# Expert weights loaded as fp16 by converting transfers on GpSimd's queue, in an attention and mixture-of-experts kernel

## The chip, the cores and the metric

One NeuronCore of a Trainium2 chip runs the whole program. Its engines are named here as the profile names them: PE (TensorE; PEld is its weight load), DVE (VectorE), ACT (ScalarE), POOL (GpSimd) and SP (SyncE, which only issues transfers here). Each works through its own instructions in order and waits on semaphores for the others. The metric is the device time of one execution in microseconds (us); lower is better.

## The reference

A cross attention between 512 tokens and 32 state rows for each of 8 x 8 (batch, head) pairs, then a dense mixture of 8 experts whose token weights come from eight rounds of Sinkhorn normalisation:

```python
scores = scale * x @ state.T                 # per batch and head, S=512, Ns=32, D=64
xread = softmax(scores) @ state
sread = softmax(scale * state @ x.T) @ x
x = concat([xread, sread])                   # as 4352 tokens x 512
P = exp(x @ w_gate - max)                    # 4352 x 8
for _ in range(8):
    P /= P.sum(1) + 1e-9; P /= P.sum(0) + 1e-9; P *= N / E
out = sum(P[:, e] * (relu(x @ w1[e]) @ w2[e]) for e in range(8))   # w1: 512x1024, w2: 1024x512
```

Inputs and output are fp32. The weights of one expert are 2 MB (w1) and 2 MB (w2); all matmuls of the kernel on large operands take fp16.

## The kernel before

The 4352 tokens are nine blocks: eight of 512 (the xread rows of one batch) and one of 256 (all sread rows). xread is never formed for the experts: aT holds the attention weights, the state is kept as a block-diagonal bdT, and for each expert and batch `project` multiplies bdT by w1 into V, so that the first expert layer is V times aT ("hidden", tile hps).

The program has two stages.

*First stage.* Attention of all batches, the gate, Sinkhorn, all of expert 0, and the first layer of expert 1 for its first two blocks are described as operations (`Op`) with a rank (a due time), the engines that may run each with planned durations, and what they depend on. `issue` (L48) plans by list scheduling: it repeatedly takes the operation that can start first by the plan, lower rank first among equals, and emits it. That fixes the order of instructions on every engine, SP's and POOL's queues too; at run time semaphores alone decide when each runs. The due times are `due_x` (L354, attention, for each half batch), `due_e` (L355, blocks of expert 0) and `due_1` (L356, the start of expert 1). Rows that the text speaks of:

- x comes in 16 pieces of 512 KB (`x_st`, two buffers, L441) on SP's queue, in 1 KB runs. The two pieces of batch 0 are cast to fp16 (`x_nat`) on DVE and ACT, the others on POOL (L454).
- `weights_ops` (L463) loads an expert's weights on SP in eight fp32 pieces of 512 KB into three staging buffers (`wst`), each cast to fp16 on ACT or DVE (L376, L378: the helper `copy`). It is called for experts 0 and 1 (L496, L497). So 16 pieces, and a piece is asked for only when the cast of the third one before it is done.
- POOL also runs the normalisation of the attention weights (`normA`, L577, tile a16), one for each half batch.
- Expert 0: `project_ops` (w1 and bdT into v_ps, copied to V), `hidden_mul` (V and aT into hps), a ReLU eviction into hT, then the second layer (hT and w2 into yps) and a copy into acc. Expert 0's result stays unscaled in acc.

*Expert loop (from L874).* For experts 1 to 7 and the nine blocks, the second layer of one block is interleaved with the first layer of the next and the projection of the one after. The second layer is a Strassen-like scheme with seven products of half size: it needs differences of parts of w2 (tile T, eight subtractions on DVE an expert, L196), sums of parts of the hidden matrix (tile sm, DVE, L277 to L280), and a copy of the first product A into a PSUM tile Bseed (ACT, L323) for which PE waits. The products are accumulated into acc on DVE (L312), scaled by the token's weight. In the pass of expert 1, acc is first scaled by expert 0's weight, half on ACT (L318), half on DVE (L320).

- `load_w` (L159) is a generator that brings in the next expert's weights: each step of it issues one fp32 piece on SP into the staging pool (`moe_wst`, three buffers) and casts the piece of two steps before on ACT (L181). Ten steps bring the eight pieces; the next eight steps make one T subtraction each.
- `step` (L875) is called after each part of the work, and every sixth call takes one step of the generator. The generator starts in block 1 of an expert (L886), and what is left of it is done after block 6 (L901).
- The fp16 weights have two buffers (`moe_w`), so an expert's load waits until the one two before is no longer read.

Of the kernel before, what the change touches and what calls it, by code (L numbers as in the profile page):

```python
# [9 lines left out]
FP32 = mybir.dt.float32  # L10
# [77 lines left out]
def kernel(  # L88
# [9 lines left out]
    nc = tc.nc  # L98

    B, H, S, D = x.shape  # L100
# [53 lines left out]
    mwst = ctx.enter_context(tc.tile_pool(name="moe_wst", bufs=3))  # L154
# [4 lines left out]
    def load_w(e, engines):  # L159
# [4 lines left out]
        casts = []  # L164
        n = NKC + NFB // 2
        for k in range(n + 2):
            if k < n:
                if k < NKC:
                    st = mwst.tile([128, F], FP32, name="w1st", tag="wst")
                    nc.sync.dma_start(out=st, in_=w1r[e, :, k, :])  # L170
                    casts.append((w1h[:, k, :], st))
                else:
                    g = k - NKC
                    st = mwst.tile([128, 2, Dm], FP32, name="w2st", tag="wst")
                    nc.sync.dma_start(out=st, in_=w2r[e, :, ds(g * 2, 2), :])
                    casts.append((w2h[:, ds(g * 2, 2), :], st))
            if k >= 2:
                dst, src = casts[k - 2]
                eng = engines[(k - 2) % len(engines)]
                if eng is nc.scalar:  # L180
                    nc.scalar.copy(out=dst, in_=src)  # L181
                else:
                    eng.tensor_copy(out=dst, in_=src)
            yield
# [20 lines left out]
    axs = actx.enter_context(tc.tile_pool(name="attn_xs", bufs=2))  # L205
# [148 lines left out]
    due_x = lambda u: 10.0 + 5.54 * u  # L354
    due_e = lambda bi: 25.1 + 13.7 * bi  # L355
    due_1 = 150.0  # L356
# [29 lines left out]
    def dma(rank, kb, emit, after=(), takes=()):  # L386
        return op(rank, {"DMA": (kb / 330.0, kb / 330.0 + 2.2)}, lambda _: emit(), after, takes)

# [50 lines left out]
    for b in range(B):  # L439
        for g in range(2):  # L440
            st = slot(axs, 2, [128, H // 2, NSC * D], FP32, "x_st")  # L441
# [21 lines left out]
    def weights_ops(e, rank, on):  # L463
        w1 = slot(mw, 2, [128, NKC, F], FP16, "w1h")
        w2 = slot(mw, 2, [128, NFB, Dm], FP16, "w2h")
        wslots[e] = (w1, w2)
        for k in range(NKC + NFB // 2):
            first = k < NKC
            st = slot(mwst, 3, [128, F], FP32, "wst")

            def load(k=k, st=st):
                if k < NKC:
                    nc.sync.dma_start(out=st.tile, in_=w1r[e, :, k, :])
                else:
                    nc.sync.dma_start(out=st.tile.rearrange("p (a b) -> p a b", a=2),
                                      in_=w2r[e, :, ds((k - NKC) * 2, 2), :])

            def cast(eng, k=k, st=st):
                if k < NKC:
                    copy(eng, w1.tile[:, k, :], st.tile)  # L480
                else:
                    copy(eng, w2.tile[:, ds((k - NKC) * 2, 2), :],
                         st.tile.rearrange("p (a b) -> p a b", a=2))

            d = dma(rank + (k,), 512, load, [w_ready.get((e, k - 1))] if k == 1 else [], [st])
            takes = [w1] if k == 0 else [w2] if k == NKC else []
            before = [w_ready[e, 0]] if 0 < k < NKC else [w_ready[e, NKC]] if k > NKC else []
            w_ready[e, k] = op(rank + (k,), on, cast, [d] + before, takes, [st])

    def w1_ready(e):  # L490
        return [w_ready[e, k] for k in range(NKC)]

    def w2_ready(e):
        return [w_ready[e, k] for k in range(NKC, NKC + NFB // 2)]
# [440 lines left out]
```

## Time and profile before

| | us |
|---|---|
| median of 3 runs | 794.11 |
| lowest and highest run | 793.38, 795.03 |
| the profiled execution's own time | 794.67 |
| its span, first to last instruction | 792.9 |

| stretch of the profiled execution | from, us | to, us |
|---|---|---|
| first stage (to the Bseed start matmuls, L871) | 0 | 165.0 |
| expert loop | 165.0 | 792.9 |

The granted TensorE clock was 0.995 over the span. The groups of weight casts, as busy time and number of instructions:

| casts | engine | busy us | count |
|---|---|---|---|
| w1h, w2h in the loop (L181) | ACT | 25.2, 25.1 | 24, 24 |
| w1h, w2h in the first stage (L376) | ACT | 5.3, 4.2 | 5, 4 |
| w1h, w2h in the first stage (L378) | DVE | 2.1, 4.2 | 3, 4 |

SP's queue carries 51.14 of the 52.46 MB that are moved. Median times from issue to landing of a 512 KB piece: 5.1 us for x_st, 6.1 us for wst in the first stage, 3.6 us for the pieces in the loop. In lines of the profile, "xN" is the number of instructions in a group, the first two numbers of a line of the timeline are start and duration in us, and a bracket at the end tells how long the engine was idle before and what ended it. A window's line gives the busy time in it of PE, PEld, DVE, ACT and POOL, with the instructions in brackets, then PE's clock, the share of time that the DMA engines were busy, and GB/s. A busy time of PE counts a matmul with its latency, so that PE can be "busy" and not at its peak.

### The profile page before, as it was taken

The numbers are of one execution on the slowest core, as the hardware profiler recorded it, in microseconds if no ns is written. First come the engines' busy times: TensorE is split into PE (matmuls) and PEld (weight loads), VectorE is DVE, ScalarE is ACT, GpSimd is POOL, SyncE is SP. The second block draws the span as 40 slices with busy tenths as digits, with TensorE's granted clock in tenths as the row PEclk, the third lists the DMA queues.
The fourth block names the chain that finished last, engine by engine and source line by source line (L and its number), as shares of the span: only waits on it lengthen the run. The fifth ranks groups of instructions, "written<-read, shape, count | busy, mean of one in ns | idle before, by whom it ended". The sixth has DMA issues, their size and how long they took to land.

```text
span 792.9 us, 16564 instructions
## 1 busy us (share of the span) xinstructions
PE 764.5 (96%) x6593; PEld 514.2 (65%) x6593; DVE 648.8 (82%) x1603; ACT 566.7 (71%) x1072; POOL 39.5 (5%) x80
## 2 busy tenths in 40 slices
PE   4899999989999999999999999999999999999996
PEld 3455554556667666766667666766667766767675
DVE  7898877787898888978788888978788888978885
ACT  5787776568977688577866688578866688576662
POOL 1543210000000000000000000000000000000000
PEclk9999999999999999999999999999999999999999
DMA  8874000002400033001410033001400030002233
GB/s 280 288 253 138 1 2 1 1 1 64 125 28 1 1 104 111 1 2 54 129 33 2 1 107 107 1 2 54 133 28 2 1 107 28 1 24 97 95 107 134
DMA packets 29535, 52.46 MB, mean 66 GB/s; under 512 B 4625, under 2 KB 12817, under 8 KB 29457
## 3 DMA queue, kind: packets, MB, share of 16 engines
q1 hardware_dynamic: 28368, 51.14, 20.3%
q8 instruction: 51, 0.84, 0.4%
q10 hardware_dynamic: 1088, 0.26, 0.2%
q14 instruction: 28, 0.22, 0.1%
HBM read 42.48 MB, written 8.91 MB: 65 GB/s over the span
## 4 chain that ended last, share of the span: by engine, by line
PE 63%; DVE 4%; ACT 2%; issue 0%; DVEq 0%
PE hps L252 22%; PE Bseed L298 16%; PE E L298 11%; PE A L298 10%; PE v_ps L237 3%; DVE acc L312 2%; ACT Hm L271 2%; DVE sm L277 1%; ACT w2h L181 1%; DVE sm L280 0%; DVE Hm L278 0%; DVE T L196 0%; DVE sm L279 0%; ACT w1h L181 0%; DVE acc L320 0%
## 5 line engine op out<-in xcount | busy, mean ns | idle before, releaser
L271 ACT ACTIVATE Hm<-hps 128x512 f16<-128x512 f32 (+1 forms) x488 | 262.3, 575 | 149.8 <-PE hps L252 138.9
L298 PEld LDWEIGHTS <-Hm 128*128 128x128 f16 x1904 | 185.4, 98 | 74.4 <-issue 3.9
L252 PE MATMUL hps<-aT,V 128*128 128x512 f16 x864 | 230.5, 379 | 0.0
L312 DVE SCALAR_TENSOR_TENSOR acc<-Bseed,Pmat,acc 128x256 f32<-128x256 f32 x357 | 156.9, 479 | 57.1 <-PE Bseed L298 53.6
L298 PEld LDWEIGHTS <-sm 128*128 128x128 f16 x1428 | 134.4, 98 | 54.9 <-DVE sm L277 24.4
L298 PE MATMUL Bseed<-T,Hm 128*128 128x256 f16 x952 | 124.5, 273 | 2.7 <-DVE acc L312 2.5
L298 PE MATMUL A<-w2h,Hm 128*128 128x256 f16 x952 | 126.1, 273 | 0.5
L252 PEld LDWEIGHTS <-V 128*128 128x128 f16 x864 | 84.5, 98 | 44.4
L241 ACT CAST V<-v_ps 128x512 f16<-128x512 f32 x216 | 111.0, 608 | 0.0
L312 DVE SCALAR_TENSOR_TENSOR acc<-E,Pmat,acc 128x256 f32<-128x256 f32 x238 | 104.4, 478 | 5.4 <-PE E L298 1.0
L277 DVE TENSOR_TENSOR sm<-Hm 128x512 f16<-128x512 f16 (+1 forms) x122 | 49.9, 409 | 21.6 <-ACT Hm L271 20.8
L298 PE MATMUL E<-T,sm 128*128 128x256 f16 x476 | 64.4, 274 | 0.7
L781 PE MATMUL yps<-w2h,hT 128*128 128x512 f16 x272 | 64.6, 379 | 0.0
L312 DVE SCALAR_TENSOR_TENSOR acc<-A,Pmat,acc 128x256 f32<-128x256 f32 x119 | 52.4, 479 | 15.0 <-PE A L298 14.9
L298 PE MATMUL Bseed<-T,sm 128*128 128x256 f16 x476 | 62.3, 272 | 2.3 <-ACT Bseed L323 2.3
L298 PE MATMUL E<-w2h,sm 128*128 128x256 f16 x476 | 62.3, 273 | 0.0
L278 DVE TENSOR_TENSOR Hm<-Hm 128x512 f16<-128x512 f16 (+1 forms) x122 | 50.0, 410 | 4.2
L280 DVE TENSOR_TENSOR sm<-Hm,sm 128x512 f16<-128x512 f16 (+1 forms) x122 | 50.0, 410 | 4.2
L279 DVE TENSOR_TENSOR sm<-sm,Hm 128x512 f16<-128x512 f16 (+1 forms) x122 | 49.1, 403 | 0.0
L323 ACT COPY Bseed<-A 128x512 f32<-128x512 f32 (+1 forms) x63 | 34.7, 552 | 18.7 <-PE A L298 15.6
L781 PEld LDWEIGHTS <-hT 128*128 128x128 f16 x272 | 24.8, 98 | 27.5 <-issue 2.6
L746 PE MATMUL hps<-aT,V 128*128 128x512 f16 x160 | 41.1, 389 | 0.4
(114 smaller groups left out, 626.1 us busy)
## 6 DMA issues: line engine op xcount, KB each, us to landing
w1st<-in_moe_w_dram SPq DMA_DIRECT2D x24, 512.0 KB, 3.6
w2st<-in_moe_w_dram SPq DMA_DIRECT2D x24, 512.0 KB, 3.6
x_st<-in_x_dram SPq DMA_DIRECT2D x16, 512.0 KB, 5.1
wst<-in_moe_w_dram SPq DMA_DIRECT2D x16, 512.0 KB, 6.1
out_dram<-acc SPq DMA_DIRECT2D x32, 256.0 KB, 3.1
out_dram<-acc SPq DMA_DIRECT2D x8, 64.0 KB, 1.7
st_st<-in_state_dram ACTq DMA_DIRECT2D x4, 64.0 KB, 3.2
st_st<-in_state_dram SPq DMA_DIRECT2D x4, 64.0 KB, 3.0
```

Of the source, the lines that this page charges most:

```text
L241: nc.scalar.copy(out=V[:, q, cols], in_=ps[q])
L252: nc.tensor.matmul(out, lhs, rhs, start=(k == 0), stop=(k == len(terms) - 1))
L271: nc.scalar.activation(out=Hm[:, i, j, :tn], in_=hps[:, :tn], func=AF.Relu)
L277: nc.vector.tensor_add(s1, a21, a22)
L278: nc.vector.tensor_sub(a21, a11, a21)
L279: nc.vector.tensor_sub(s2, s1, a11)
L280: nc.vector.tensor_sub(s4, a12, s2)
L298: nc.tensor.matmul(dst[:, c], lhs(j, c), rhs[:, j], start=first and c == 0 and j == 0, stop=(j == NJ - 1), skip_group_check=True)
L312: nc.vector.scalar_tensor_tensor(out=dst, in0=src[:, c], scalar=p[:, k], in1=dst, op0=ALU.mult, op1=ALU.add)
L323: nc.scalar.copy(out=Bb[:, :nk], in_=A[:, :nk])
L746: nc.tensor.matmul(ps.tile[:, :tn], lhs, rhs, start=(k == 0), stop=(k == len(terms) - 1))
L781: nc.tensor.matmul(yps.tile, hT[fb].tile[:, ds(tk * 128, 128)], w2h[:, fb, :], start=(fb == 0), stop=(fb == NFB - 1))
```

## The change

All weight loads move from SP's queue to POOL's, as 1 MB transfers that read fp32 and write fp16 directly into w1h and w2h: four an expert, 32 in all, in place of 64 of 512 KB. The staging pool and all 64 casts are gone. In the first stage, `dma16` books an issue on POOL (1.0 us in the plan) and then a transfer. The x staging gets a third buffer. The due times are others: 5.77 for 5.54, 27.5 and 14.7 for 25.1 and 13.7, and `due_1` 100 for 150; expert 1's weights are due at 50 (120 before). In `load_w`, four steps issue the four transfers, three steps do nothing, and the T subtractions follow.

The list scheduler makes of it, as the built program shows: SP's queue holds the state, then all 16 pieces of x with nothing between, and at the end the output. POOL's queue begins, after the masks, with five transfers and no wait between them: expert 0's first half of w1, expert 0's first half of w2, expert 1's first half of w1, expert 1's first half of w2, and then expert 0's second half of w1. (In the plan a second half may be issued only when the first half's transfer is done, a first half at once.) Then come the first normalisation, expert 0's second half of w2, and the x cast of batch 1; the two second halves of expert 1 stand among later x casts. On PE, the same matmuls as before stand in another order: expert 1's first layer for its two blocks no longer ends the stage, but stands among the second-layer matmuls of expert 0, twelve of which stand between the last two Sinkhorn sums.

```diff
--- before.py
+++ after.py
@@ -151,7 +151,6 @@
     outx = [out[b * SB:b * SB + S, :].rearrange("(p sc) d -> p sc d", sc=NSC) for b in range(B)]
     outs = [out[b * SB + S:(b + 1) * SB, :] for b in range(B)]
 
-    mwst = ctx.enter_context(tc.tile_pool(name="moe_wst", bufs=3))
     mw = ctx.enter_context(tc.tile_pool(name="moe_w", bufs=2))
     gsb = ctx.enter_context(tc.tile_pool(name="gate_sb", bufs=2))
     vpool = ctx.enter_context(tc.tile_pool(name="vpool", bufs=3))
@@ -161,26 +160,13 @@
         w1h = mw.tile([128, NKC, F], FP16, name="w1h", tag="w1h")
         w2h = mw.tile([128, NFB, Dm], FP16, name="w2h", tag="w2h")
         w16[e] = (w1h, w2h)
-        casts = []
-        n = NKC + NFB // 2
-        for k in range(n + 2):
-            if k < n:
-                if k < NKC:
-                    st = mwst.tile([128, F], FP32, name="w1st", tag="wst")
-                    nc.sync.dma_start(out=st, in_=w1r[e, :, k, :])
-                    casts.append((w1h[:, k, :], st))
-                else:
-                    g = k - NKC
-                    st = mwst.tile([128, 2, Dm], FP32, name="w2st", tag="wst")
-                    nc.sync.dma_start(out=st, in_=w2r[e, :, ds(g * 2, 2), :])
-                    casts.append((w2h[:, ds(g * 2, 2), :], st))
-            if k >= 2:
-                dst, src = casts[k - 2]
-                eng = engines[(k - 2) % len(engines)]
-                if eng is nc.scalar:
-                    nc.scalar.copy(out=dst, in_=src)
-                else:
-                    eng.tensor_copy(out=dst, in_=src)
+        for k in range(2):
+            nc.gpsimd.dma_start(out=w1h[:, ds(2 * k, 2)], in_=w1r[e, :, ds(2 * k, 2), :])
+            yield
+        for k in range(2):
+            nc.gpsimd.dma_start(out=w2h[:, ds(k * NJ, NJ)], in_=w2r[e, :, ds(k * NJ, NJ), :])
+            yield
+        for _ in range(3):
             yield
         if e:
 
@@ -202,7 +188,7 @@
 
     mh = ctx.enter_context(tc.tile_pool(name="moe_h", bufs=10))
     actx = ExitStack()
-    axs = actx.enter_context(tc.tile_pool(name="attn_xs", bufs=2))
+    axs = actx.enter_context(tc.tile_pool(name="attn_xs", bufs=3))
     axp = actx.enter_context(tc.tile_pool(name="attn_x", bufs=3))
     axt = actx.enter_context(tc.tile_pool(name="attn_xt", bufs=2))
     asb = actx.enter_context(tc.tile_pool(name="attn_sb", bufs=2))
@@ -351,9 +337,9 @@
 
 
     ops = []
-    due_x = lambda u: 10.0 + 5.54 * u
-    due_e = lambda bi: 25.1 + 13.7 * bi
-    due_1 = 150.0
+    due_x = lambda u: 10.0 + 5.77 * u
+    due_e = lambda bi: 27.5 + 14.7 * bi
+    due_1 = 100.0
     rings = {"bank": Ring(8)}
     EVICT16 = {"DVE": (0.36, 0.48), "ACT": (0.50, 0.66)}
     EVICT32 = {"ACT": (0.50, 0.66), "DVE": (0.62, 0.74)}
@@ -385,6 +371,10 @@
 
     def dma(rank, kb, emit, after=(), takes=()):
         return op(rank, {"DMA": (kb / 330.0, kb / 330.0 + 2.2)}, lambda _: emit(), after, takes)
+
+    def dma16(rank, kb, emit, after=(), takes=(), uses=()):
+        asked = op(rank, {"POOL": (1.0, 1.0)}, lambda _: emit(), after, takes, uses)
+        return op(rank, {"DMA": (kb / 330.0, kb / 330.0 + 2.2)}, lambda _: None, [asked])
 
 
     st_bd = spl.tile([128, B, NQ, 128], FP16, name="st_bd")
@@ -438,7 +428,7 @@
     x_ready = []
     for b in range(B):
         for g in range(2):
-            st = slot(axs, 2, [128, H // 2, NSC * D], FP32, "x_st")
+            st = slot(axs, 3, [128, H // 2, NSC * D], FP32, "x_st")
 
             def load(b=b, g=g, st=st):
                 nc.sync.dma_start(
@@ -460,41 +450,29 @@
     w_ready = {}
     t_ready = []
 
-    def weights_ops(e, rank, on):
+    def weights_ops(e, rank):
         w1 = slot(mw, 2, [128, NKC, F], FP16, "w1h")
         w2 = slot(mw, 2, [128, NFB, Dm], FP16, "w2h")
         wslots[e] = (w1, w2)
-        for k in range(NKC + NFB // 2):
-            first = k < NKC
-            st = slot(mwst, 3, [128, F], FP32, "wst")
-
-            def load(k=k, st=st):
-                if k < NKC:
-                    nc.sync.dma_start(out=st.tile, in_=w1r[e, :, k, :])
+        for k in range(NKC):
+            def load(k=k):
+                if k < 2:
+                    nc.gpsimd.dma_start(out=w1.tile[:, ds(2 * k, 2)], in_=w1r[e, :, ds(2 * k, 2), :])
                 else:
-                    nc.sync.dma_start(out=st.tile.rearrange("p (a b) -> p a b", a=2),
-                                      in_=w2r[e, :, ds((k - NKC) * 2, 2), :])
-
-            def cast(eng, k=k, st=st):
-                if k < NKC:
-                    copy(eng, w1.tile[:, k, :], st.tile)
-                else:
-                    copy(eng, w2.tile[:, ds((k - NKC) * 2, 2), :],
-                         st.tile.rearrange("p (a b) -> p a b", a=2))
-
-            d = dma(rank + (k,), 512, load, [w_ready.get((e, k - 1))] if k == 1 else [], [st])
-            takes = [w1] if k == 0 else [w2] if k == NKC else []
-            before = [w_ready[e, 0]] if 0 < k < NKC else [w_ready[e, NKC]] if k > NKC else []
-            w_ready[e, k] = op(rank + (k,), on, cast, [d] + before, takes, [st])
+                    h = ds((k - 2) * NJ, NJ)
+                    nc.gpsimd.dma_start(out=w2.tile[:, h], in_=w2r[e, :, h, :])
+
+            w_ready[e, k] = dma16(rank + (k,), 1024, load, [w_ready[e, k - 1]] if k % 2 else [],
+                                  [] if k % 2 else [w2 if k else w1], [w2 if k > 1 else w1] if k % 2 else [])
 
     def w1_ready(e):
-        return [w_ready[e, k] for k in range(NKC)]
+        return [w_ready[e, k] for k in range(2)]
 
     def w2_ready(e):
-        return [w_ready[e, k] for k in range(NKC, NKC + NFB // 2)]
-
-    weights_ops(0, (3.0, 4), {"ACT": (0.95, 1.10), "DVE": (0.75, 0.95)})
-    weights_ops(1, (due_1 - 30.0, 0), {"ACT": (0.95, 1.10), "DVE": (0.75, 0.95)})
+        return [w_ready[e, k] for k in range(2, 4)]
+
+    weights_ops(0, (3.0, 4))
+    weights_ops(1, (due_1 - 50.0, 0))
 
 
     a_ready, su_ready, gates, turned = {}, [], [], []
@@ -521,7 +499,7 @@
                               [t] + ([xt_ready[0]] if hp else []),
                               [] if hp else [xT], [ps] + ([xT] if hp else []))
         for q in range(NQ):
-            r = lambda n, b=b, q=q: (due_x(2 * b + q) + 0.1 * 5.54 * n,)
+            r = lambda n, b=b, q=q: (due_x(2 * b + q) + 0.1 * 5.77 * n,)
             psA = psum([128, NSC, 4, Ns], FP32, "psA")
             psB = psum([128, S], FP32, "psB")
             mxA, sA, rA = rows("mxA"), rows("sA"), rows("rA")
@@ -768,8 +746,8 @@
             def act(eng, tn=tn, ps=ps, h=h):
                 relu(eng, h.tile[:, :tn], ps.tile[:, :tn])
 
-            t = op((due_e(bi) + 0.05 * 13.7 * fb,), {"PE": (0.44, 0.62)}, mul, deps, [ps], held)
-            h_ready.append(op((due_e(bi) + 0.05 * 13.7 * fb,), EVICT32, act, [t], [h], [ps]))
+            t = op((due_e(bi) + 0.05 * 14.7 * fb,), {"PE": (0.44, 0.62)}, mul, deps, [ps], held)
+            h_ready.append(op((due_e(bi) + 0.05 * 14.7 * fb,), EVICT32, act, [t], [h], [ps]))
             hT.append(h)
         for tk in range(tn // 128):
             yps = psum([128, Dm], FP32, "yps")
@@ -782,14 +760,14 @@
                                          start=(fb == 0), stop=(fb == NFB - 1))
 
                 fbs = range(half * NJ, half * NJ + NJ)
-                last = op((due_e(bi) + 13.7 * (0.4 + 0.075 * (2 * tk + half)),), {"PE": (0.87, 1.04)}, mul,
-                          [h_ready[fb] for fb in fbs] + w2_ready(0)[2 * half:2 * half + 2] + [last],
+                last = op((due_e(bi) + 14.7 * (0.4 + 0.075 * (2 * tk + half)),), {"PE": (0.87, 1.04)}, mul,
+                          [h_ready[fb] for fb in fbs] + w2_ready(0)[half:half + 1] + [last],
                           [] if half else [yps], [hT[fb] for fb in fbs] + ([yps] if half else []))
 
             def keep(eng, k=t0 // 128 + tk, yps=yps):
                 copy(eng, acc[:, k, :], yps.tile)
 
-            op((due_e(bi) + 13.7 * (0.4 + 0.075 * (2 * tk + 1)),), EVICT32, keep, [last], [], [yps])
+            op((due_e(bi) + 14.7 * (0.4 + 0.075 * (2 * tk + 1)),), EVICT32, keep, [last], [], [yps])
 
 
     pools1 = {}
```

## The prediction

> **What bounds the kernel now.** I read the utilisation page first, then five-microsecond windows, then the order in time of the places where PE is not fed.
>
> ```profile
> span 792.9 us, 16564 instructions
> PE 764.5 (96%) x6593; PEld 514.2 (65%) x6593; DVE 648.8 (82%) x1603; ACT 566.7 (71%) x1072; POOL 39.5 (5%) x80
> ...
> DMA  8874000002400033001410033001400030002233
> ```
>
> PE is the bound, so a change on ACT, DVE or the queues is worth only the PE idle time that it removes or adds. The DMA row shows two regimes: nearly full in the first three slices (60 us), then bursts with wide gaps. The windows (busy time of PE, PEld, DVE, ACT, POOL, granted clock, DMA share, GB/s) say where PE is idle.
>
> ```profile
> 5.00:10.00 5.00, 2.95 (x24) 2.52 (x25) 3.86 (x13) 1.81 (x5) 0.00 (x0) 1.00 0.98 312
> 10.00:15.00 5.00, 3.65 (x58) 2.68 (x57) 3.59 (x8) 3.46 (x9) 0.00 (x0) 1.00 1.04 393
> 15.00:20.00 5.00, 3.34 (x35) 1.95 (x33) 4.13 (x11) 3.55 (x8) 2.50 (x5) 1.00 0.90 306
> 20.00:25.00 5.00, 3.43 (x63) 1.99 (x56) 4.92 (x12) 4.52 (x10) 2.42 (x5) 0.95 0.90 259
> 25.00:30.00 5.00, 4.64 (x30) 2.38 (x28) 3.97 (x11) 3.85 (x10) 1.52 (x4) 0.71 0.99 338
> ...
> 60.00:65.00 5.00, 5.00 (x32) 2.34 (x30) 4.19 (x12) 4.12 (x10) 1.13 (x1) 1.00 0.01 3
> ...
> 155.00:160.00 5.00, 4.27 (x18) 1.80 (x19) 4.79 (x12) 4.91 (x11) 0.00 (x0) 1.00 0.00 0
> 160.00:165.00 5.00, 4.02 (x20) 1.71 (x18) 4.69 (x15) 5.00 (x12) 0.00 (x0) 1.00 0.00 0
> ```
>
> Up to 20 us PE idles 10.1 us (5 of them before the first data), from 20 to 45 us another 4.1; from 60 to 155 us it is full, and there freeing ACT or DVE gains nothing. Just before the expert loop (which starts at 165.0) it idles again, with ACT full. In the loop the tell-tale is the distance between successive projections (L237), one for each token block:
>
> ```profile
> 175.45 0.63 PE L237 MATMUL v_ps<-w1h,bdT 64*32 64x512 f16 x16
> 185.68 0.62 PE L237 MATMUL v_ps<-w1h,bdT 64*32 64x512 f16 x16
> 197.22 0.63 PE L237 MATMUL v_ps<-w1h,bdT 64*32 64x512 f16 x16
> ...
> 185.40 1.04 ACT L181 CAST w1h<-w1st 128x1024 f16<-128x1024 f32 x1
> 186.34 1.33 ACT L318 ACTIVATE acc<-acc,Pmat 128x512 f32<-128x512 f32 x2
> 187.57 0.58 ACT L323 COPY Bseed<-A 128x512 f32<-128x512 f32 x1
> ...
> 188.21 1.03 PE L298 MATMUL Bseed<-T,sm 128*128 128x256 f16 x8 [0.93 <-ACT Bseed L323]
> ```
>
> A block takes 10.23 us undisturbed and 11.54 us when a cast stands in ACT's queue ahead of the copy that PE waits for.
>
> **The change, part by part.** All terms are against the profiled execution: 792.9 us of span and 1.8 us around it, 794.67 us in all, which is 0.56 us above the median of 794.11, inside the spread of 793.38 to 795.03.
>
> *Casts of experts 2 to 7 gone (48 on ACT, 25.2 + 25.1 = 50.3 us).* Almost all of it is hidden, because PE is full. What shows: in the pass of expert 1, two blocks of 11.54 and 11.55 us instead of 10.23. Without the cast, the scaling pair would start at 185.40 and the copy end about 0.95 us earlier, leaving 0.14 us of wait; at two places that is 2 x (1.31 - 0.14) = **-2.3**, bounds 0 (another wait fills in) and -2.6. In the later passes the spacings show seven blocks of 10.46: 7 x 0.23 = **-1.6**, bounds 0 and -1.6. At 239.79 a block takes 10.51 against 9.85 elsewhere; the chain shows DVE doing three T subtractions (L196) in a row there. The new generator reaches them three steps earlier, so I take half of 0.66: **-0.3**, bounds 0 and -0.66.
>
> *The loop's loads, now on POOL.* 24 issues of 1 MB replace 48 of 0.5 MB on SP. POOL's last compute instruction comes before the loop, so nothing but other weight loads queues behind one that waits for its buffer. The new wait is DVE's: T subtractions need w2h, and accumulations and the s-sums that PE needs queue behind them. A generator step comes each sixth work step, 15 steps to a 10.23 us block, thus each 4.1 us. The second half of w2h is asked for at 12.3 us, and read six steps later, at about 36.9. So 4 MB in 36 us, some 115 GB/s, suffices; SP's loads of the same weights ran at 312 to 393 GB/s when queued. Price **0**, and if the rate fell below 115, 4 MB at 100 would be 5 us late per expert.
>
> *The 16 casts in the first 165 us gone* (rows of 5.3, 4.2, 4.2 and 2.1: 15.8 us on ACT and DVE). From 60 us on they cost nothing. Earlier, the cast at 13.25 holds ACT 1.05 us while xT's copy and an exponential wait for it; others at 17.91 and 20.01 hold the chain of block 0 by about 0.4 each. But that chain will wait for data (below), so I take less than these 1.9: **-1.5**, bounds 0 and -4.1 (all idle time from 20 to 45 us; 1.4 of it lies where the clock fell to 0.71).
>
> *Schedule at the end of the first stage.* Before, all 32 hidden matmuls of expert 1's first two blocks stand at 155.03 to 164 us behind ACT's evictions. From their starts and the undisturbed pace (16 in 3.6 us) I read gaps of 1.4, 0.3 and 1.2 = 2.9 us. In the new PE order these stand earlier, between second-layer matmuls, and the stage ends with 12 of the latter between the last two Sinkhorn sums. An iteration takes 3.5 us by the rows at 141 to 145 us, 12 matmuls 2.6, so 0.9 is given back: **-2.0**, bounds 0 and -2.9.
>
> *The start: weights beside x, and a new order among the weights.* This is the risk. Before, SP issues the state, two x pieces of 0.5 MB, then weights in turn with x, as fast as three staging buffers come free; expert 0's w1 is cast by 19 us, and the first hidden matmul starts at 24.74. Now POOL asks for five 1 MB loads with no wait, from 1.9 us on, and the second half of expert 0's w1 is the fifth, behind 2 MB of expert 1. On PE's new order the projections for block 0, and behind them block 1's scores, wait for it. No row has two large queues in flight. Lower bound: both arrive as early as now, **0**. Otherwise by bytes: three x buffers hold 1.6 MB, so 5.2 + 1.6 = 6.8 MB go by before w1 is whole. At the mean of the three full windows (312, 393, 306: 337 GB/s) that takes 20.3 us; from 3.3 us, w1 is there at 23.6. The x pieces: if each 1 KB x packet takes turns with a 4 KB (w1) or 2 KB (w2) packet, the second comes with the third weight load, after 3.1 + 1.0 MB, at 15.6 instead of 9.6; with some 7.5 us from cast to aT (copies and transposes 2.4, scores 0.4, reductions, exponential and reciprocal 3.0, normalisation 1.1, semaphores), the aT transposes ahead of the projections end at 23.5. Both lead to projections at about 24, and hidden matmuls 3.9 us later (4.2 in the rows before, less part of two casts): 27.9, **+3.2**, which I take. Upper bound at the slowest full window, 259 GB/s: w1 at 29.6, hidden matmuls at 33.5, +8.8.
>
> *POOL's issues* stand ahead of its first normalisation, which ran at 16.5 us; five of them in 14.6 us leave 2.9 each free. SP's took 0.33 to 0.54. Price **0**; at twice the room it would be +14.6, which no row supports. A sixth stands before block 1's x cast and costs what one issue takes, covered by the wait for w1. The third x buffer only lets SP ask earlier.
>
> The Trainium skill, "SBUF — State Buffer", section "Who interferes with whom", speaks against the change: descriptors for a load issued on GpSimd are written by GpSimd, and VectorE in a two-port mode locks it out; the page tells of 0.62 us becoming 3.1. The row: DVE is 3.86 of 5 us busy at 5 to 10 us. By the page, five loads each 2.5 us late would bring w1 some 12 us later and the time to about 802, an estimate from that page; no row here shows such a load.
>
> **Sum:** -2.3 - 1.6 - 0.3 - 1.5 - 2.0 + 3.2 = -4.5, so 794.67 - 4.5 = **790.2 us**.
>
> **The rivals.** (1) *Slower: expert 0's w1 comes too late.* The forecast's gains without the start are 7.7 us, so it decides once hidden matmuls start after 32.4, that is w1 after 28.5, or 6.8 MB in 25.2 us: below 270 GB/s. If converting loads and x together reach two thirds of 337, 225, w1 is there at 33.5, hidden matmuls at 37.4, +12.7: 794.67 - 7.7 + 12.7 = **799.7 us**; at half, 168, w1 comes at 43.8 and it is 810. For it: the break-even lies inside the measured windows (259 to 393), PE's order is fixed, and no row shows what converting costs. Against: such a load reads the same bytes and writes half, and larger transfers need fewer issues.
>
> (2) *Nothing measurable:* the loop gains 4.2, but the first stage's idle time is latency: casts and tail 0, start +3.2: 794.67 - 1.0 = **793.7 us**. For it: PE's waits at the start name state and x transfers and short chains, not casts alone.
>
> (3) *The queues don't hurt each other:* start 0, casts -4.1: 794.67 - 4.2 - 2.0 - 4.1 = **784.4 us**. Against: the DMA engines are 0.9 to 1.04 busy up to 30 us, so what weights gain, x loses.
>
> **How the numbers follow.** Forecast 0.42, rival 1 0.38, rival 2 0.12, rival 3 0.08. The predicted time is the forecast's. The range takes in rival 3 and most of rival 1, between its two thirds and its half: 783 to 806; the forecast's own is 786 to 796 by the start's bounds. A measurement of this kernel tells 0.2%, 1.6 us, from no change. Forecast (but for its upper edge) and rival 3 are faster, rival 2 the same, rival 1 slower: 0.47, 0.15, 0.38.
>
> **What would show it.** After: no spacings of 11.5 or 10.46 us between projections in the loop; hidden matmuls of expert 0 starting at 27 to 29 us (after 32.4 is rival 1, at 25 rival 3); x's second piece landing at 14 to 17 us; the loop starting at 164 to 165. I am wrong if a weight load takes over 7 us per MB, if DVE waits for w2h in the loop, if POOL's issues hold its normalisations, or if PE idles after 60 us where it was full.

## The result, and the profile after

The changed kernel takes 797.55 us (median of 5 runs, 796.95 to 798.56) against 793.47 us of the kernel before (5 runs, 793.38 to 795.03): a ratio of 1.0049, with a 95% interval of 1.0038 to 1.006. It is slower by some 4 us; 790.2 had been forecast. The profiled execution has a span of 796.8 us (792.9 before) and took 798.56 us.

The page of the changed kernel: utilisation, DMA row, queues, issues (q0 is POOL's queue, q1 SP's):

```profile
span 796.8 us, 16437 instructions
...
PE 763.1 (96%) x6593; PEld 513.6 (64%) x6593; DVE 640.6 (80%) x1593; ACT 520.2 (65%) x1018; POOL 62.4 (8%) x112
...
DMA  9664000042000500060002400060003300002233
...
q0 software_dynamic: 12800, 16.78, 12.7%
q1 hardware_dynamic: 15056, 17.58, 7.0%
...
L164 POOL DMA_DIRECT2D w1h<-in_moe_w_dram x12 | 8.5, 714 | 453.2 <-PE hps L238 407.0
...
w1h<-in_moe_w_dram POOLq DMA_DIRECT2D x16, 512.0 KB, 7.1
w2h<-in_moe_w_dram POOLq DMA_DIRECT2D x16, 512.0 KB, 7.4
x_st<-in_x_dram SPq DMA_DIRECT2D x16, 512.0 KB, 5.1
...
wg_st<-in_moe_w_gate_dram SPq DMA_DIRECT2D x1, 16.0 KB, 19.1
```

DVE lost 8.2 us of work and ACT 46.5, and PE has the same 6593 matmuls in a span that is 3.9 us longer, so PE idles more. The page counts a converting load by the bytes it writes (512 KB for 1 MB read). One row stands out: 16 KB of w_gate, which landed 5.1 us after issue before, now take 19.1. The row of the kernel before:

```profile
wg_st<-in_moe_w_gate_dram SPq DMA_DIRECT2D x1, 16.0 KB, 5.1
```

Where PE idles, the windows of the changed kernel tell (columns as before: PE, PEld, DVE, ACT, POOL, clock, DMA share, GB/s):

```profile
5.00:10.00 5.00, 0.29 (x1) 0.10 (x1) 1.56 (x4) 0.00 (x0) 0.52 (x1) 1.00 1.10 204
10.00:15.00 5.00, 1.78 (x15) 1.52 (x15) 1.40 (x4) 1.56 (x3) 0.00 (x0) 1.00 1.14 241
15.00:20.00 5.00, 1.32 (x8) 0.89 (x9) 1.19 (x5) 0.00 (x0) 0.00 (x0) 1.00 1.24 232
20.00:25.00 5.00, 0.80 (x31) 0.79 (x31) 0.51 (x2) 1.32 (x4) 0.00 (x0) 1.00 1.14 315
25.00:30.00 5.00, 3.66 (x37) 2.09 (x33) 3.74 (x9) 2.27 (x5) 0.00 (x0) 1.00 0.22 71
```

From 5 to 25 us PE is busy 4.19 us, where it was busy 13.37; the DMA engines are full, and DVE and ACT too are idle most of the time. At 25 the flood, as the five weight loads in flight at once are called from here on, is over (DMA share 0.22), and only then does the chain of block 0 start. The timeline of the same stretch (start, duration, and in the bracket the idle time before and what ended it) names what was late:

```profile
10.75 0.87 DVE L364 CAST st_bd<-st_st 32x512 f16<-32x512 f32 x2 [4.09 <-DMA st_st<-in_state_dram]
...
14.87 0.90 DVE L364 CAST x_nat<-x_st 128x256 f16<-128x256 f32 x4 [2.23 <-DMA x_st<-in_x_dram]
...
20.16 1.32 ACT L362 CAST x_nat<-x_st 128x256 f16<-128x256 f32 x4 [5.96 <-DMA x_st<-in_x_dram]
...
23.97 0.18 DVE L399 CAST wgh<-wg_st 128x32 f16<-128x32 f32 x1 [7.40 <-DMA wg_st<-in_moe_w_gate_dram]
24.20 1.02 PE L419 MATMUL G_ps<-wgh,bdT 128*64 128x8 f16 x32 [7.67 <-DVE wgh L399]
...
36.09 0.63 PE L700 MATMUL v_ps<-w1h,bdT 64*32 64x512 f16 x8
39.94 2.79 PE L724 MATMUL hps<-aT,V 128*128 128x512 f16 x10
```

The same four places in the timeline of the kernel before: the second x piece is cast, the gate's G matmuls, the first projection and the first hidden matmul start.

```profile
9.62 1.34 ACT L376 CAST x_nat<-x_st 128x256 f16<-128x256 f32 x4
...
10.06 1.02 PE L429 MATMUL G_ps<-wgh,bdT 128*64 128x8 f16 x32 [0.18 <-DVE wgh L409]
...
19.44 0.63 PE L722 MATMUL v_ps<-w1h,bdT 64*32 64x512 f16 x8
...
24.74 2.72 PE L746 MATMUL hps<-aT,V 128*128 128x512 f16 x6
```

Now PE stands 7.67 us at the G matmuls for w_gate, which in PE's fixed order stand ahead of block 0's scores. The projections do *not* wait for w1: they have no bracket, and the fifth load, w1's second half, had landed at 24.2 us (asked for at 4.79, and 19.4 to landing, the longest of the w1 loads).

In the loop the projections now stand at these times (timeline of the changed kernel):

```profile
176.07 0.62 PE L223 MATMUL v_ps<-w1h,bdT 64*32 64x512 f16 x16
183.42 0.62 PE L223 MATMUL v_ps<-w1h,bdT 64*32 64x512 f16 x16
193.65 0.62 PE L223 MATMUL v_ps<-w1h,bdT 64*32 64x512 f16 x16
204.02 0.62 PE L223 MATMUL v_ps<-w1h,bdT 64*32 64x512 f16 x16
```

No 11.5 and no 10.46 are left: blocks take 10.23, and 10.37 in expert 1's pass. So the span of the profiled execution splits like this: the first hidden matmul of expert 0 comes 15.2 us later (24.74 to 39.94), the way from there to the loop is 5.6 us shorter (140.3 to 134.7), and the loop 5.7 us shorter (627.9 to 622.2). 15.2 - 5.6 - 5.7 = +3.9.

### The profile page after: what moved, and what is told of

It reads as the page before. It is cut to its first block, busy times and chain, and to the rows that moved or that the text cites. A ratio compares the mean times of both kernels' runs of the same rounds, so it can differ in the third digit from the quotient of the medians.

```text
span 796.8 us, 16437 instructions
## 1 busy us (share of the span) xinstructions
PE 763.1 (96%) x6593; PEld 513.6 (64%) x6593; DVE 640.6 (80%) x1593; ACT 520.2 (65%) x1018; POOL 62.4 (8%) x112
## 3 DMA queue, kind: packets, MB, share of 16 engines
q0 software_dynamic: 12800, 16.78, 12.7%
q1 hardware_dynamic: 15056, 17.58, 7.0%
q10 hardware_dynamic: 1088, 0.26, 0.2%
## 4 chain that ended last, share of the span: by engine, by line
PE 66%; DVE 3%; ACT 1%; issue 0%
PE hps L238 23%; PE Bseed L284 17%; PE E L284 12%; PE A L284 11%; PE v_ps L223 3%; DVE acc L298 1%; DVE sm L263 1%; ACT Hm L257 1%; DVE sm L266 0%; DVE Hm L264 0%; DVE sm L265 0%; DVE T L182 0%; ACT Bseed L309 0%
## 5 line engine op out<-in xcount | busy, mean ns | idle before, releaser
L257 ACT ACTIVATE Hm<-hps 128x512 f16<-128x512 f32 (+1 forms) x488 | 261.6, 572 | 181.5 <-PE hps L238 166.1
L238 PE MATMUL hps<-aT,V 128*128 128x512 f16 x864 | 230.7, 379 | 0.0
L309 ACT COPY Bseed<-A 128x512 f32<-128x512 f32 (+1 forms) x63 | 34.5, 548 | 19.4 <-PE A L284 18.2
L164 POOL DMA_DIRECT2D w1h<-in_moe_w_dram x12 | 8.5, 714 | 453.2 <-PE hps L238 407.0
## 6 DMA issues: line engine op xcount, KB each, us to landing
wg_st<-in_moe_w_gate_dram SPq DMA_DIRECT2D x1, 16.0 KB, 19.1
```

What stands on the lines that cost most here:

```text
L238: nc.tensor.matmul(out, lhs, rhs, start=(k == 0), stop=(k == len(terms) - 1))
L257: nc.scalar.activation(out=Hm[:, i, j, :tn], in_=hps[:, :tn], func=AF.Relu)
L309: nc.scalar.copy(out=Bb[:, :nk], in_=A[:, :nk])
```

## The experiments

Eleven kernels were run, each measured against runs of the kernel before on the same chip, whose medians were 793.4 to 793.67. Times in us; "second x", "G" and "hidden" are the starts of the cast of batch 0's second x piece, of the G matmuls and of expert 0's first hidden matmul in the profiled execution; "loop from" is the start of the Bseed matmuls at the end of the first stage, "rest" the way from hidden to there, "loop" from there to the end of the span. These columns are of one execution of each kernel, which lies up to 1.2 us off the median in the last column.

| kernel | second x | G | hidden | loop from | rest | loop | median (range) | ratio to before, 95% |
|---|---|---|---|---|---|---|---|---|
| before | 9.62 | 10.06 | 24.74 | 165.0 | 140.3 | 627.9 | 793.47 (793.38-795.03) | |
| after | 20.16 | 24.20 | 39.94 | 174.6 | 134.7 | 622.2 | 797.55 (796.95-798.56) | 1.0049 [1.0038, 1.006] |
| p_wg | 18.32 | 15.16 | 33.05 | 167.7 | 134.7 | 622.1 | 792.57 (791.61-793.21) | 0.9989 [0.998, 0.9998] |
| p_order | 18.61 | 19.03 | 34.77 | 169.5 | 134.7 | 622.1 | 792.81 (792.04-793.84) | 0.9993 [0.9983, 1.0002] |
| order_wg | 18.27 | 17.59 | 33.33 | 168.1 | 134.7 | 622.1 | 791.49 (790.38-793.01) | 0.9976 [0.9963, 0.9989] |
| p_small | 13.89 | 15.51 | 30.95 | 165.9 | 135.0 | 622.1 | 790.66 (789.82-791.15) | 0.9968 [0.9956, 0.998] |
| p_hold | 9.19 | 9.63 | 36.45 | 171.1 | 134.7 | 622.2 | 795.12 (793.74-795.8) | 1.0022 [1.0012, 1.0031] |
| p_hold_order | 9.17 | 9.61 | 24.51 | 159.9 | 135.4 | 622.1 | 783.91 (783.76-784.53) | 0.9883 [0.9868, 0.9897] |
| ho_wg | 11.38 | 12.07 | 27.82 | 162.5 | 134.7 | 622.2 | 786.3 (785.32-786.46) | 0.9905 [0.9888, 0.9921] |
| loop_only | 9.63 | 10.07 | 24.70 | 163.0 | 138.3 | 623.8 | 789.85 (788.61-790.8) | 0.9961 [0.9947, 0.9975] |
| dues_on_before | 9.43 | 9.88 | 25.38 | 165.5 | 140.1 | 626.1 | 793.3 (792.28-793.81) | 0.9998 [0.9988, 1.0007] |
| ho_olddues | 9.12 | 9.57 | 24.91 | 162.6 | 137.7 | 623.8 | 788.22 (788.15-788.44) | 0.9941 [0.9926, 0.9956] |
| hold_order | 9.61 | 10.05 | 26.81 | 166.1 | 139.3 | 622.1 | 791.0 (790.0-791.69) | 0.9968 [0.9955, 0.9981] |

Read the column "rest" first: wherever the changed kernel's PE order was kept, it is 134.7 to 135.4, from a start at 24.5 to one at 39.9. A late start is not made up for: each us at the first hidden matmul is a us at the loop.

### p_wg: w_gate asked for first

Its transfer is issued on ACT's queue ahead of all others; the plan, and so every order on PE, DVE and ACT, stays that of the changed kernel.

```diff
-    wgd = dma((0, 2), 16, lambda: nc.sync.dma_start(
-        out=wg_st, in_=moe_w_gate.rearrange("(kc p) e -> p kc e", p=128)))
+    nc.scalar.dma_start(out=wg_st, in_=moe_w_gate.rearrange("(kc p) e -> p kc e", p=128))
+    wgd = dma((0, 2), 16, lambda: None)
```

> As the changed kernel, but the 16 KB of w_gate are asked for first, on ACT's queue, in place of fourth on SP's; the order of all compute instructions is the same. Theory 1 (small transfers and x are starved by 5 MB of weights asked for at once): w_gate no longer lands at 24 us, the G matmuls start near 17 instead of 24.2, the second x piece still lands near 20; first hidden matmul of expert 0 near 34 instead of 39.9, time about 794. Theory 2 (expert 0's w1 is late because it is the fifth load): nothing moves, 797.5. Theory 3 (the new planned order of instructions loses the time, whatever the transfers do): 797.5.

Measured: 792.57 us, 5.0 less than the changed kernel; hidden at 33.05 in place of 39.94. Moving 16 KB of 52 MB takes back the whole loss, about as theory 1 had it. What binds next stands in the timeline of p_wg:

```profile
15.16 1.02 PE L419 MATMUL G_ps<-wgh,bdT 128*64 128x8 f16 x32 [0.18 <-DVE wgh L399]
...
18.32 1.32 ACT L362 CAST x_nat<-x_st 128x256 f16<-128x256 f32 x4 [3.47 <-DMA x_st<-in_x_dram]
...
29.20 0.63 PE L700 MATMUL v_ps<-w1h,bdT 64*32 64x512 f16 x8
```

The G matmuls are free of w_gate, and x's second piece, at 18.32, is the last to come. From its cast to the projections it is 10.9 us, and 3.85 more to the first hidden matmul.

### p_order: expert 0's loads first

POOL issues expert 0's two halves of w1 and its first of w2, then, behind its first normalisation, the second half of w2 and expert 1's. Only the order of the loads changes (the new lines; "..." stands for unchanged ones, and `turn_in` takes the place of `load` in the call of `dma16`):

```diff
+    line = [(e, k) for e in range(2) for k in range(4)]
+    later = {}
...
+            def turn_in(e=e, k=k, load=load):
+                later[e, k] = load
+                while line and line[0] in later:
+                    later.pop(line.pop(0))()
```

> As the changed kernel, but POOL's first weight loads stand in the order expert 0 w1, w1, w2, (first normalisation), w2, then expert 1; three loads instead of five are asked for at once; no other engine's order changes. Theory 1: state, x and w_gate are still late, but behind 3 MB, not 5: second x piece and w_gate near 15, first hidden matmul near 32, time about 793. Theory 2: w1 lands near 14 instead of 24 and the hidden matmuls follow it, near 25 to 28: time 788 to 790. Theory 3: 797.5.

Measured: 792.81 us, hidden at 34.77. It looks as if w1's place had cost 5 us; but the G matmuls, which have nothing to do with w1, moved from 24.20 to 19.03, by the same 5.2 us. With three loads in flight in place of five, the small transfers beside them get through sooner. In both kernels the first hidden matmul comes 15.74 us after the G matmuls. So it is theory 1 that fits, and theory 2 (25 to 28) does not.

### order_wg: both of these

> Weight loads issued in the order of expert 0 first (w1, w1, w2, then w2 and expert 1's) and w_gate asked for on ACT's queue ahead of all; nothing held back, so x and the state still share the DMA engines with the weights. Theory (two bounds at the start, each of which alone keeps block 0 late: small transfers on SP's queue, and expert 0's w1 as fifth load): with w1 second of the loads and w_gate early, what is left is x's second piece (about 18.5 us by the run with the order alone), so first hidden matmul at 30 to 32, stage end 134.7 later at 165 to 167, median 789 to 791. Rival (either bound is enough, so the two edits' gains of 6.9 and 5.2 us at the first hidden matmul add up): 27.8, stage end 162.5, median 786. Rival (w1's place decides nothing once w_gate is early): 33, as with w_gate alone, 792.5.

Measured: 791.49 us, hidden at 33.33, against 33.05 of p_wg. Beside an early w_gate, w1's place gave nothing at the first hidden matmul: the second rival is what happened, and the theory, which put two equal bounds at the start, fell. The 1.1 us between the medians of the two kernels (their ranges overlap) is not explained by that; their profiled executions, 791.61 and 791.95, do not show it.

### p_hold: the weights wait for the small transfers

POOL reads one column of each state piece, of batch 0's two x pieces and of w_gate (eleven tiny copies into a tile that nobody uses) before it issues any weight load. The loads' order is the changed kernel's. The part of the edit that waits (`early` holds the loads asked for so far):

```diff
+    def landed(tile_ap):
+        wait_for.append(tile_ap)
+        if len(wait_for) == 11:
+            for n, ap in enumerate(wait_for):
+                nc.gpsimd.tensor_copy(out=seen[ds(0, ap.shape[0]), ds(n, 1)], in_=ap)
+            for emit in early:
+                emit()
```

> As the changed kernel, but POOL reads one column of the state, of both first x pieces and of w_gate (eleven tiny copies) before it issues its first weight load, so that no weights are in flight until these have landed; order of everything else unchanged. Theory 1: state, x and w_gate land by 9 us as before the change, weights start then, w1 is whole near 29, first hidden matmul near 33, time about 793. Theory 2: w1 comes 5 us later than now, so the hidden matmuls too, near 43, and the time is about 800. Theory 3: 797.5.

Measured: 795.12 us. State, x and w_gate are as early as before the change, and now PE does wait for w1, which is still the fifth load, and is asked for 7.8 us later (12.60 in place of 4.79). The time lies between those of theories 1 and 2. The timeline of p_hold:

```profile
9.63 1.02 PE L440 MATMUL G_ps<-wgh,bdT 128*64 128x8 f16 x32 [0.30 <-DVE wgh L420]
...
21.51 0.61 PE L723 MATMUL v_ps<-w1h,bdT 64*32 64x512 f16 x1
32.60 0.62 PE L723 MATMUL v_ps<-w1h,bdT 64*32 64x512 f16 x7 [10.48 <-DMA w1h<-in_moe_w_dram]
```

So w1's place is a second bound, hidden behind the first in the changed kernel; the hold itself moves it back by those 7.8 us.

### p_hold_order: the hold, and expert 0's loads first

> Both: loads held until state, x and w_gate have landed, and expert 0's weights first. Theory 1 and 2 together: x by 9, w1 whole near 17 to 18, first hidden matmul near 26, loop starting near 166, time about 789. Theory 1 alone: no better than the held kernel by more than 1 us. Theory 3: 797.5.

Measured: 783.91 us, 13.6 less than the changed kernel and a ratio of 0.9883 [0.9868, 0.9897] to the kernel before, 5 us better than expected; hidden at 24.51, as early as before the change (24.74). It is the fastest of all kernels here. The timeline of p_hold_order:

```profile
9.61 1.02 PE L440 MATMUL G_ps<-wgh,bdT 128*64 128x8 f16 x32 [0.18 <-DVE wgh L420]
...
21.49 0.63 PE L731 MATMUL v_ps<-w1h,bdT 64*32 64x512 f16 x8
24.51 2.33 PE L755 MATMUL hps<-aT,V 128*128 128x512 f16 x10
```

No bracket ahead of the projections: w1, first of the loads, is there although it was held until 9.3 us. The hold alone gave 2.4 us (p_hold), the order alone 4.7 us (p_order, where the flood got smaller too), both together 13.6: the bounds lie one behind the other. The expectation was too high behind the hidden matmul: it put some 140 us (26 to 166) from there to the loop, and they are 135.4.

### ho_wg: as p_hold_order, with w_gate first on ACT's queue

> As the run with the weights held behind the small transfers and expert 0's loads first (783.91), with w_gate asked for on ACT's queue ahead of all. Theory (with the weights held, w_gate was there at 9.4 us and nothing waited for it): within 0.2% of 783.9, first hidden matmul at 24.3 to 24.8. Rival (w_gate still stands in the way of the state pieces and x's second piece on SP's queue): first hidden matmul up to 0.5 us earlier, 783.4; it could not be told from the theory by the time, only by the state's and x's landing in the trace.

Measured: 786.3 us, slower by 2.4, which neither side expected. The second x piece is cast at 11.38 in place of 9.17 and the G matmuls start at 12.07: with w_gate in front, POOL sees the last two state pieces at 8.1 us, where it was through with all eight at 6.3, and x lands after them. What w_gate is to a queue, the row of ACT's queue in p_wg tells: 1616 packets where the changed kernel has 1088, so w_gate is 528, as many as 512 KB of x. Whichever queue it is on, somebody stands behind it; behind x, where p_hold_order has it, nobody waits.

### p_small: the weights in runs of 1 KB

Each 1 MB load is cut by columns into two of 0.5 MB, so that a contiguous run of weights is 1 KB in place of 4 (w1) or 2 (w2). Nothing is held and the loads' order stays. The new lines:

```diff
+                for c in range(2):
+                    if k < 2:
+                        f = ds((2 * k + c) * 256, 256)
+                        nc.gpsimd.dma_start(out=w1.tile[:, :, f], in_=w1r[e, :, :, f])
+                    else:
+                        h, f = ds((k - 2) * NJ, NJ), ds(c * 256, 256)
+                        nc.gpsimd.dma_start(out=w2.tile[:, h, f], in_=w2r[e, :, h, f])
```

> As the changed kernel, but the first stage's weight loads are cut by columns into transfers of 0.5 MB with runs of 1 KB in memory, in place of 4 KB and 2 KB; as many bytes, order of all engines unchanged, twice the issues on POOL. Theory 1 (queues take turns packet by packet, so what stands beside 4 KB packets gets a small share): x and w_gate get a larger share, second x piece near 12 to 14 instead of 20.2, w_gate near 16 instead of 24, first hidden matmul near 33, time about 792. Rival (x is late for another reason, such as a fixed priority of POOL's queue or the 5 MB being served first): second x piece and w_gate stay within 2 us of 20.2 and 24, time 797 or more.

Measured: 790.66 us, 6.9 less than the changed kernel, with the same bytes beside x. The timeline of p_small:

```profile
13.89 1.32 ACT L362 CAST x_nat<-x_st 128x256 f16<-128x256 f32 x4 [2.47 <-DMA x_st<-in_x_dram]
15.28 0.18 DVE L399 CAST wgh<-wg_st 128x32 f16<-128x32 f32 x1 [2.76 <-DMA wg_st<-in_moe_w_gate_dram]
```

x is there 6.3 us earlier, and w_gate 1.4 us behind x in place of 3.8. This is what queues that take turns packet by packet do: a small packet waits for one of the other queue, whatever its size. An estimate by turns of two queues at the 337 GB/s of the prediction: 528 packets (counted under ho_wg) of 1 KB of x, each with 1 KB of weights, take 3.2 us, and 528 of 32 bytes of w_gate 1.7; from the first x piece's cast (10.81) to the second's it is 3.1 us, and 1.4 from there to w_gate's. The Trainium skill, "DMA: Bandwidth & Descriptors", section "Queues, rings and completion order", states it: each DMA engine goes round its queue rows a packet at a time. Whether a turn is one run of bytes or several, no run here shows. The run has one impurity: POOL issues twice as many loads, and waits at 9.34 us for an earlier one, so the flood itself is also somewhat thinner at the start.

### loop_only: the kernel before, with the new loop loads alone

The first stage is that of before; `load_w` is that of after.

> The first stage of the kernel before, unchanged, and the changed kernel's generator in the expert loop. Theory 1 (the loop gains by itself what the traces show between the start matmuls of Bseed and the end, 627.9 against 622.15 us): time about 5.7 us below the kernel before, 787.7. Rival: 1.7 us of that gain belongs to the first block of the loop and comes from the new order at the end of the first stage, so the casts are worth only 4.1: 789.3.

Measured: 789.85 us, 3.6 less than before; the loop is 623.8 us long, 4.1 less than before's 627.9, so the rival was right. The spacings of 11.54 us have become 10.38 and 10.37 (projections at 183.68, 194.06 and 204.43). The fewer casts and the loads on POOL are worth this by themselves, and no other wait took their place: where spacings of 10.46 stood in the later passes, they are 10.23.

### dues_on_before: the kernel before, with the new due times alone

> The kernel before with nothing but the new due times (5.77; 27.5 and 14.7; 100; expert 1's weights due at 50). From the first hidden matmul of expert 0 to the end of the first stage the kernel before takes 140.3 us, the changed one and four variants of it 134.7 to 135.4. Theory 1 (those 5.6 us come from the new order of instructions, mainly at the stage's end): this stretch falls to about 135 here, time about 788. Rival (they come from the 16 casts that are gone): it stays near 140, time 793 or more.

Measured: 793.3 us, no difference that can be told (0.9988 to 1.0007): the rival's time. The loop is 1.8 us shorter (626.1), "rest" is the same (140.1), and the first hidden matmul comes 0.6 us later.

### ho_olddues: p_hold_order with the old due times

> The kernel with held loads and expert 0's weights first, but with the due times of the kernel before. Theory 1 (the 5.6 us come from the new order): first hidden matmul still near 24.5, the stretch from there to the end of the stage near 140, time about 789. Rival (they come from the casts that are gone): stretch near 135, time about 784.

Measured: 788.22 us, 4.3 more than p_hold_order: "rest" 137.7 in place of 135.4, loop 623.8 in place of 622.1. A "rest" of 137.7 lies between theory and rival. So the new due times are worth some 4 us together with the new loads; on the kernel before the medians show nothing of it, though the loop got 1.8 us shorter there too.

### hold_order: the hold told to the planner

The reads become operations of the plan (four here, one of them over all state pieces) and the loads of expert 0 go first in it, so that the list scheduler lays out all engines anew.

> The hold and expert 0's loads first, this time told to the planner, which then lays out the orders of all engines anew for it. Theory (the start is bound by DMA, and what is left of the stage by PE, so a plan that knows of the hold can fill PE while it waits but not end the stage much earlier): stage end 158 to 161, median 782 to 786. Rival (the order of the changed kernel was good by luck of its due times; another plan loses what the order gained, 2.5 us): 786 to 789.

Measured: 791.0 us, 7.1 more than p_hold_order, worse than the theory and the rival had it. The start is 2.3 us later (hidden at 26.81) and "rest" 139.3. Between 40 and 60 us PE is busy 16.63 us, in p_hold_order 19.84, and the longest of PE's waits there is 3.1 us for a normalisation on POOL. In this execution the granted clock also fell to 0.50 between 25 and 30 us, where p_hold_order has 1.00. How the loss divides between the new plan's moves and the clock was not taken apart.

## Why the prediction was wrong

*The step that failed* is "The start: weights beside x, and a new order among the weights": +3.2 was taken, with an upper bound of +8.8, and it measured +15.2. The forecast had two legs, both ending at projections at about 24 us. The leg over w1 was right: 23.6 worked out, 24.2 measured, and PE did not wait for it. The leg over x failed in three ways, which add up from the 27.9 forecast to the 39.94 measured:

- x's second piece was put at 15.6 and was cast at 20.16: +4.6. The text gave x a turn against each weight packet, but counted only x's own packets. SP's four state pieces stand in front of x, in smaller packets: ACT's queue, which carries the other four and nothing else, has 1088 in its row, 272 for a piece of 64 KB (256 runs and 16 more). By the same count a piece of x, eight times the size, has 512 runs of 1 KB and 16 more, 528. So the four state pieces on SP's queue, 1088, are about as many packets as the two x pieces behind them, 1056. The trace of the changed kernel goes by this count: the last state piece is cast at 10.75, x's pieces at 14.87 and 20.16, w_gate at 23.97, so that some 528 packets took 4.1, 5.3 and 3.8 us, whether they were 512 KB or 16. That the state costs x the 4.6 us is worked out from this; no run moves the state alone.
- From that piece to the projections 8.4 us were taken (15.6 to 24) from the sum of single instructions; p_wg, where x alone decides, shows 10.9: +2.5. The sum has one chain from cast to aT. In PE's new order the transposes of both half batches stand ahead of the projections: in p_wg the first half batch's aT transposes end 6.8 us after the cast (25.13), but the second normalisation starts at 27.44, 4.1 us after the first, and the projections follow its transposes. The last leg, 3.9 from projection to hidden matmul, was right (3.85).
- w_gate was left out altogether, and PE's G matmuls stand ahead of the scores. It follows x on SP's queue, 528 packets beside the weights', and came when the flood was over, at 24.0: the remaining 39.94 - 20.16 - 10.9 - 3.85 = +5.0. p_wg moves w_gate alone and shows the term: its hidden matmul comes 6.9 us earlier, 1.8 of them from x's second piece (18.32) and 5.0 from w_gate. (That the medians, too, differ by 5.0 is chance; the profiled executions, 798.56 and 791.61, differ by 7.0.)

The profile of before had the warning: its issue row of w_gate, 16 KB in 5.1 us, said that this transfer takes as long as 512 KB of x (5.1), and its group sits on PE's path at 10.06 us.

*What held, and by how much.* Loop casts: -2.3 - 1.6 - 0.3 = -4.2 forecast, -4.1 measured (loop_only); the spacing of 10.23 + 0.14 = 10.37 in expert 1's pass came out to the hundredth. The loads of the loop: priced 0, and 0 measured, with no wait of DVE for w2h. A weight load does take over 7 us per MB (7.1 and 7.4), which the text had named as a sign of being wrong; in the loop it is latency with nobody waiting. POOL's issues: priced 0; they take 0.70 to 0.84 us each, and the first normalisation waits 24.7 us for DVE's reciprocal, not for them. First-stage casts: -1.5 forecast; "rest" went from 140.3 (138.3 in loop_only, the same first stage) to 137.7 in ho_olddues, -0.6 to -2.6, but the hold and the new loads are in this difference too; no run takes away the casts alone. The schedule at the end of the stage: -2.0 forecast; the new due times took "rest" from 137.7 to 135.4 (p_hold_order), -2.3, and it is 134.7 in the changed kernel, with another -1.7 at the entry of the loop (623.8 to 622.1) that was not priced: in the changed kernel the way from the loop's first projection to its third is 17.58 us (176.07 to 193.65), where it was 19.26 before (166.42 to 185.68). So the parts other than the start gained 11.3 by the profiled executions (5.6 + 5.7), where 7.7 had been forecast; the start took all of it back, and 3.9 more. The remark beside the bound of the first-stage casts, that 1.4 us of PE's idle time lies where the clock fell to 0.71, does not fit that window, in which PE idles 0.36; nothing but that remark hangs on it.

*The rivals.* Rival 1, slower because expert 0's w1 comes too late, had the sign and nearly the time (799.7), but not the mechanism: order_wg and the missing bracket at the projections show that w1 was not waited for. Its bound is real, one layer deeper (p_hold, 10.48 us). Its supposition, that converting loads and x together reach two thirds of 337 GB/s or less, is refuted: by it w1 would have been there at 33.5 or later, and it was at 24.2. The queue rows agree: by the time that their packets took, 33.55 MB in 12.7% of 796.8 us are 332 GB/s of fp32 read, against 51.14 MB in 20.3% of 792.9 us, 318, before. Rival 2 was wrong in that the parts are far from nothing, they nearly cancel. Rival 3, 784.4, is what the change is worth once the start is mended: p_hold_order measured 783.91. That the sum is so near is partly luck: its start cost nothing, as the rival had it, but "rest" gave 4.9 us where the rival has 6.1, and the loop 5.8 where it has 4.2. Its reason (queues don't hurt each other) is false.

The rule weighed in the prediction, that DVE may starve GpSimd's writing of descriptors, is not seen: a load's issue takes 0.714 us in the mean in the loop (w1h), with DVE busy 80% of the span, and 0.70 to 0.84 at the start, where DVE casts the state beside three of them. No row tells whether DVE ran in the mode that the page speaks of.

*Open:* the share of each move in the new order's 4 us, the 1.1 us between order_wg and p_wg, and the 2 us by which "rest" differs between before and loop_only, which run the same first stage. The last may be no more than spread: the profiled execution of before took 1.2 us more than its kernel's median, that of loop_only 1.2 less.

## What to carry to other kernels

When a flood of large transfers is moved to a queue of its own, list every small transfer that the first chain needs, masks, gates and state too, and count it in packets, not in bytes: here, with two queues in flight, 16 KB in runs of 32 bytes were held up nearly as long as 512 KB in runs of 1 KB. Let the flood start only when the small ones have landed, and put in it first what is needed first; here the two together were worth 13.6 us, and each alone 2.4 and 4.7. And when a plan's order is fixed ahead of time, look at everything that PE must do *before* the instruction you are timing.

## What the runs showed of the hardware

- A 16 KB transfer counts 528 packets and landed 19.1 us after its issue beside five converting loads on another queue, and 5.1 us after it in the kernel before and in p_hold_order.
- No loss of rate is seen from converting fp32 to fp16 in the transfer: by the time of their packets 332 GB/s read, against 318 on SP's queue before. Issuing one takes POOL 0.70 to 0.84 us.
- The granted clock fell between 20 and 35 us in the kernel before (0.71), in loop_only (0.67) and in hold_order (0.50), and not in the others. It does not explain why "rest" is longer before than after: dues_on_before has a clock of 1.00 there and the same "rest" as the kernel before. What it cost hold_order is open.
